# A Fourier mixing and feed-forward kernel: half-row products moved ahead of the slot's feed-forward product, one block scaled by a matmul, moved slots, and another setup

## The chip, the cores and the metric

The kernel runs on one core of one Trainium2 chip. The metric is the device time of one execution in microseconds (us), the median of several runs. Lower is better. A core has five engines that matter here: TensorE (PE in the profile; its weight loads are PEld), VectorE (DVE), ScalarE (ACT), GpSimd (POOL) and SyncE (SP), which issues DMA transfers. GpSimd issues DMA transfers too. Each engine works through its own list of instructions, and waits on semaphores where an operand comes from another engine.

## The reference, cut to what matters

Each of 8 sequences of 3008 rows and 256 features is filtered in the frequency domain. The result goes row by row through a normalization and a gated feed-forward layer of width 1536.

```python
def _attn_ref(x, filt_r, filt_i):            # x: 8 x 3008 x 256
    X = np.fft.rfft(x, axis=1)
    F = (filt_r + 1j * filt_i)[None, :, :]   # 1505 x 256
    Y = X * F
    return np.fft.irfft(Y, n=x.shape[1], axis=1)

def _moe_ref(x, w_gate, w_val, w_out, rms_g):  # x: 24064 x 256
    rms = np.sqrt(np.mean(x * x, axis=-1, keepdims=True) + 1e-06)
    xn = x / rms * rms_g
    g = xn @ w_gate                            # 256 -> 1536
    silu = g * (1.0 / (1.0 + np.exp(-g)))
    val = xn @ w_val
    return silu * val @ w_out                  # 1536 -> 256
```

## The kernel before

A transform of length 3008 = 47 x 64 is done as matmuls with constant tables: a_unit (length 64), b_unit (length 47, followed by the products with the filter), bi_unit (inverse of b) and n_unit (inverse of a, whose result is normalized). Data goes through DRAM between the units to be reordered (z_tmp between a and b, g_tmp between bi and n). Matmuls write to banks of PSUM, each a pool of one or two buffers; bank 3 and bank 0 have one buffer each.

For sequences 2 to 7 the filter products are made from half the rows at a time: s1 is one full product on VectorE (L248), then swap_unit makes two half-row products (L274 and L272) from the same PSUM bank, after which GpSimd adds the two (L278).

The units and the normalization:

```python
# the mixing of one sequence: a (first transform), b (second, with the filter), bi and n (inverse)
        pool, tag = ((psM, "mx"), (psG, "pg"), (psV, "pv"), (psB, "mb"), (psO, "po1"), (psO, "po0"))[i]
# ... cut ...
    def b_mm(b, i):
        ps = bank(3 if b else (0, 3, 4, 5)[i % 4], "psb").rearrange("p (a d) -> p a d", a=2)
# ... cut ...
    def b_unit(b, i, ps=None):
        if ps is None:
            ps = b_mm(b, i)
        f1, f2 = filt(2 * i, 2)
        if b:
            s1 = late_p["sp"].tile([P, 2, D], FP16, tag="s1", name="s1")
            s2 = late_p["sp"].tile([P, 2, D], FP16, tag="s2", name="s2")
            if b > 1:
                nc.vector.tensor_tensor(out=s1, in0=ps, in1=f1, op=ALU.mult)
                st[b]["s"][i] = (s1, s2, ps, f2)
                return
# ... cut ...
        eng = nc.vector
        if (i in (5, 8, 11, 14)) if b else (i in (3, 7, 10, 13)):
            eng = nc.gpsimd
# ... cut ...
            nc.scalar.activation(out=v, in_=ps, func=AXT.Copy)
            ps = v
        eng.tensor_tensor(out=s1, in0=ps, in1=f1, op=ALU.mult)
        eng.tensor_tensor(out=s2, in0=ps, in1=f2, op=ALU.mult)
        st[b]["s"][i] = (s1, s2)

    def swap_unit(b, i, h):
        s1, s2, ps, f2 = st[b]["s"][i]
        a, e = slice(HALF * h, HALF * h + HALF), slice(HALF - HALF * h, P - HALF * h)
        if h:
            nc.vector.tensor_tensor(out=s2[a], in0=ps[e], in1=f2[e], op=ALU.mult)
        else:
            nc.vector.scalar_tensor_tensor(out=s2[a], in0=ps[e], scalar=-1.0, in1=f2[e],
                                           op0=ALU.mult, op1=ALU.mult)
        if h:
            s = late_p["ssp"].tile([P, 2, D], FP16, tag="s", name="s")
            nc.gpsimd.tensor_tensor(out=s, in0=s1, in1=s2, op=ALU.add)
            st[b]["s"][i] = (s,)

    def bi_unit(b, i):
# ... cut ...
                nc.tensor.matmul(ps[:, u, :], wi_at(q, 2 * i + u), ss[q][:, u, :],
                                 start=(q == 0), stop=(q == n - 1))
# ... cut ...
# normalization: squares, their sum over the 256 features, 1/sqrt, broadcast over partitions
    def q_unit(b, m):
# ... cut ...
                nc.tensor.matmul(ps[:, q:q + 1], sq[:, dh, ts(q, P)], ones,
                                 start=(dh == 0), stop=(dh == 1))
# ... cut ...
        rho = up.tile([P, 4], FP32, tag="rho", name="rho")
        nc.vector.tensor_scalar(out=u[:, 0:n], in0=ps[:, 0:n], scalar1=1.0 / D, scalar2=1e-6 * Y_SCALE * Y_SCALE,
                                op0=ALU.mult, op1=ALU.add)
        nc.gpsimd.tensor_tensor(out=rho[:, 0:n], in0=u[:, 0:n], in1=mhalf[:, 0:n], op=ALU.pow)
        if b or m > 1:
            nc.gpsimd.dma_start(r_d[b, m, 0:n * P].rearrange("(p q) -> p q", q=n), rho[:, 0:n])
# ... cut ...
    def rho_load(b, m):
        rb = late_p["rp"].tile([P, 4 * P], FP32, tag="rb", name="rb")
        w = nq(b, m) * P
        nc.sync.dma_start(rb[:, 0:w], r_d[b, m, 0:w].partition_broadcast(P))
        st[b]["u"][m] = rb

    def scale_apply(m, bk):
        hl = st[0]["u"].pop(m)
        y = st[0]["y"].pop(m)
        ps = bank(bk, "psr")
        for q in range(4):
            for e in range(2):
                nc.tensor.matmul(ps[:, ts(q, P)], hl[:, e, q:q + 1].to_broadcast([P, P]), ident,
                                 start=(e == 0), stop=(e == 1))
        xn = xnp.tile([P, 2, 512], FP16, tag="xn", name="xn")
        for dh in range(2):
            nc.vector.tensor_tensor(out=xn[:, dh, :], in0=ps, in1=y[:, dh, :], op=ALU.mult)
        st[0]["xn"][m] = xn

    def xn_unit(b, m):
# ... cut ...
        nc.gpsimd.tensor_tensor(out=xv, in0=yv, in1=rv.unsqueeze(1).to_broadcast([P, 2, n, P]),
                                op=ALU.mult)
        st[b]["xn"][m] = xn
```

The feed-forward layer is a list of 576 items, 12 for each of 6 blocks of 512 rows in each of 8 sequences. gv makes the two products of an item (pg and pv), ScalarE the sigmoid-weighted sg, VectorE the product hh; down adds hh times w_out into po, two slots later:

```python
    def gv(b, m, jt):
# ... cut ...
        for ps, wt in ((pg, wg), (pv, wv)):
            for dt_ in range(2):
                nc.tensor.matmul(ps[:, 0:w], wt[:, dt_, ts(jt, P)], xn[:, dt_, 0:w],
                                 start=(dt_ == 0), stop=(dt_ == 1))
# ... cut ...
        nc.scalar.activation(out=sg[:, 0:w], in_=pg[:, 0:w], func=AXT.Silu)
        nc.vector.tensor_tensor(out=hh[:, 0:w], in0=pv[:, 0:w], in1=sg[:, 0:w], op=ALU.mult)
# ... cut ...
    def down(b, m, jt):
# ... cut ...
        for s4 in range(n):
            nc.tensor.matmul(po[s4 // 2][:, s4 % 2, :], hh[:, ts(s4, P)], wo[:, jt, :],
                             start=(jt == 0 and s4 % 2 == 0),
                             stop=(jt == JT - 1 and (s4 % 2 == 1 or s4 == n - 1)))
# ... cut ...
        if jt == JT - 1:
# ... cut ...
            nc.scalar.activation(out=o3[:, 0:2, :], in_=po[0], func=AXT.Copy)
            nc.vector.tensor_copy(out=o3[:, 2:n, :], in_=po[1][:, 0:n - 2, :])
```

Everything else is laid into the slots of these items by a plan: at slot i comes gv, then the slot's planned units, then the down product of item i - 2, then the q_units.

```python
        def at(slot, fn, *a):
            todo = (late if fn == q_unit else plan).setdefault(slot, [])
            if fn in (sq_unit, swap_unit):
                todo.insert(0, (fn, a))
            else:
                todo.append((fn, a))

        def norm_plan(b, m, s0, s1, r):
            for dh in range(2):
                at((s0, s1)[dh], n_unit, b, m, dh)
                at((s0, s1)[dh] + 1, sq_unit, b, m, dh)
            for d, fn in zip(r, (q_unit, rho_load, xn_unit)):
                at(s1 + d, fn, b, m)
# ... cut ...
            b_at = [t - 26 + 4 * i for i in range(16)]
# ... cut ...
            elif b == 2:
# ... cut ...
                b_at = [72] + [71 + 3 * i for i in range(1, 16)]
                lag, t4_at = 5, 123
                n_at = [127 + 8 * m for m in range(6)]
            elif b == 3:
# ... cut ...
            for i in range(16):
                s0 = b_at[i]
                at(s0, b_unit, b, i)
                if b > 1:
                    at(s0 + 1, swap_unit, b, i, 0)
                    at(s0 + 2, swap_unit, b, i, 1)
                at(s0 + lag - (b == 2 and i == 0), bi_unit, b, i)
                if i % 2 == 1:
                    at(s0 + lag + 1, g_store, b, i // 2)
            if b + 1 < B:
                for c in range(NXC):
                    at((24, 73)[b - 1] + 2 * c if b < 3 else a_at[3 * c + 2] + 2, x_load, b + 1, c)
# ... cut ...
        for i in range(len(items) + 4):
            if i < len(items):
                gv(*items[i])
            for fn, a in plan.get(i, ()):
                fn(*a)
            if 2 <= i < len(items) + 2:
                down(*items[i - 2])
                if items[i - 2][2] == JT - 1:
                    stores[i + 1] = items[i - 2][:2]
            for fn, a in late.get(i, ()):
                fn(*a)
            if i in stores:
                o_store(*stores[i])
```

Ahead of the slots stands a setup: tables and filters are loaded, and sequence 0 is mixed without DRAM between its units. The filter parts fr and fi (4 tiles each, c = 0 to 3) are loaded into half of the partitions and copied to the other half by f_dup. t1_unit makes transposes (pt), t2_unit too (of gT); bit_unit is the inverse of b for sequence 0 (pgt, copied to gT); n_first and y_first make the first block's normalization input.

```python
    def f_dup(c, which=(0, 1)):
        for e in which:
            t = (fr, fi)[e][c]
            a, o = (0, HALF) if e else (HALF, 0)
            if c == 3:
                nc.sync.dma_start(t[a:a + HALF], t[o:o + HALF])
            elif e:
                nc.gpsimd.tensor_copy(out=t[a:a + HALF], in_=t[o:o + HALF])
            else:
                nc.scalar.activation(out=t[a:a + HALF], in_=t[o:o + HALF], func=AXT.Copy)
# ... cut ...
        for m in range(6):
            if m == 4:
                warm_up(6, 0)
            for dh in range(2):
                at_unit(m, dh)
# ... cut ...
        ps0 = {}
        for g in range(8):
            t1_unit(g)
            if g == 1:
                ps0.update((i, b_mm(0, i)) for i in range(2))
        ps0.update((i, b_mm(0, i)) for i in range(2, 4))
        f_dup(0)
        f_dup(1, (1,))
        f_dup(3)
        for i in range(16):
            if i == 6:
                f_dup(2)
            b_unit(0, i, ps0.get(i))
            if i == 3:
                f_dup(1, (0,))
            if i % 2 and i >= 5:
                bit_unit(i - 5)
                bit_unit(i - 4)
            if i == 13:
                w_load(0)
                w_load(1)
        for i in range(12, 16):
            bit_unit(i)
        t2_unit(0, 1)
        t2_unit(1, 0)
        warm_up(2, 0)
        first = n_first()
        y_first(*first, 1)
        q_unit(0, 0)
        y_first(*first, 0)
        scale_split(0)
        t2_unit(2, 0)
        t2_unit(3, 0)
        scale_apply(0, 3)
        t2_unit(4, 0)
```

Of the kernel before, what the change touches and what calls it, by code (L numbers as in the profile page):

```python
# [12 lines left out]
AXT = mybir.ActivationFunctionType  # L13
# [109 lines left out]
def kernel(  # L123
# [105 lines left out]
    def b_mm(b, i):  # L229
        ps = bank(3 if b else (0, 3, 4, 5)[i % 4], "psb").rearrange("p (a d) -> p a d", a=2)  # L230
# [7 lines left out]
        return ps  # L238

    def b_unit(b, i, ps=None):  # L240
        if ps is None:
            ps = b_mm(b, i)
# [15 lines left out]
        if (i in (5, 8, 11, 14)) if b else (i in (3, 7, 10, 13)):  # L258
# [75 lines left out]
    def q_unit(b, m):  # L334
# [12 lines left out]
        if b or m > 1:  # L347
            nc.gpsimd.dma_start(r_d[b, m, 0:n * P].rearrange("(p q) -> p q", q=n), rho[:, 0:n])
        else:
            st[b]["u"][m] = rho  # L350
# [21 lines left out]
    def y_first(y, pss, dh):  # L372
        if dh:
            nc.scalar.activation(out=y[:, dh, :], in_=pss[dh], func=AXT.Identity, scale=gsb[:, dh:dh + 1])
            return
# [3 lines left out]
    def scale_split(m):  # L379
        rho = st[0]["u"].pop(m)  # L380
# [3 lines left out]
        st[0]["u"][m] = hl  # L384

    def scale_apply(m, bk):
        hl = st[0]["u"].pop(m)
        y = st[0]["y"].pop(m)
# [8 lines left out]
        st[0]["xn"][m] = xn  # L397
# [13 lines left out]

    hh_of = {}
# [65 lines left out]
    def f_dup(c, which=(0, 1)):  # L478
        for e in which:
            t = (fr, fi)[e][c]  # L480
            a, o = (0, HALF) if e else (HALF, 0)
            if c == 3:
                nc.sync.dma_start(t[a:a + HALF], t[o:o + HALF])
            elif e:
                nc.gpsimd.tensor_copy(out=t[a:a + HALF], in_=t[o:o + HALF])
            else:
                nc.scalar.activation(out=t[a:a + HALF], in_=t[o:o + HALF], func=AXT.Copy)
# [13 lines left out]
    def t1_unit(g):  # L501
# [7 lines left out]
        pool, tag = ((psG, "pg"), (psV, "pv"))[g % 2]  # L509
# [7 lines left out]
        if g != 1:  # L517
# [75 lines left out]
    with tc.manual_schedule():  # L593
# [26 lines left out]
        for c in range(1, 4):  # L620
            nc.vector.memset(fr[c][0:HALF], 0.0)
            zero(fi[c][HALF:P])
        with nc.allow_non_contiguous_dma(reason="one gain a partition"):
            nc.sync.dma_start(gsb, moe_rms_g.rearrange("(a p) -> p a", p=P))
        for c in range(4):
            f_load(c, filt_r, fr[c], 0, nc.sync)
            f_load(c, filt_i, fi[c], HALF, nc.gpsimd if c < 3 else nc.sync)
# [4 lines left out]
        for m in range(6):  # L632
            if m == 4:
                warm_up(6, 0)
# [4 lines left out]
        ps0 = {}  # L639
        for g in range(8):  # L640
            t1_unit(g)
            if g == 1:
                ps0.update((i, b_mm(0, i)) for i in range(2))
# [169 lines left out]
```

## Time and profile before

| | |
|---|---|
| time, median of 3 | 919.47 us (918.31 to 919.63) |
| span of the profiled run | 917.9 us |
| TensorE busy | 884.3 us, 96% |
| VectorE busy | 673.8 us, 73% |
| ScalarE busy | 618.8 us, 67% |
| GpSimd busy | 391.6 us, 43% |
| DMA | 102.22 MB, mean 111 GB/s |
| granted TensorE clock, mean | 0.991 of full |
| first pg matmul of slot 0 | 48.31 us after the span's start |

The profile counts a matmul as busy from its start to a modelled end, so that matmuls overlap one another. What a stretch must take at least is better read from the number of columns that its matmuls move, and from the start-to-start time of matmuls that wait for nothing. The start of slot n is the start of the first pg matmul of item n: slot 0 at 48.31 us, slot 71 at 168.50, slot 72 at 171.64, slot 119 at 255.41, slot 120 at 256.71.

In a line of the profile, L428 is line 428 of the kernel before, an arrow as in hh<-pv,sg has the written tile at its left, and "idle before" names what ended the engine's idle time.

### The profile page before, as it was taken

The page shows a single profiled execution, that of the slowest core. Times are in us where ns is not written, and L with a number is a line of the kernel's source. Part 1 is how long each engine was busy: PE and PEld are TensorE (multiplying, and loading weights), DVE is VectorE, ACT ScalarE, POOL GpSimd, SP SyncE. Part 2 cuts the span into 40 slices and gives each one's busy share as a digit, 9 for nine tenths or more (in the row PEclk, how much of TensorE's full clock was granted, in tenths as well). Part 3 has the DMA queues.
Part 4 walks back from the last instruction along what each step waited for, and adds up shares of the span by engine and source line. Part 5 has one row for each costly group of instructions (what it writes and reads, how often), then busy time and mean ns, then how long its engine had stood idle before and what let it go on. Part 6 is the DMA issues. An engine that isn't in the chain of part 4 may idle for free.

```text
span 917.9 us, 17521 instructions
## 1 busy us (share of the span) xinstructions
PE 884.3 (96%) x6327; PEld 560.6 (61%) x6327; DVE 673.8 (73%) x1069; ACT 618.8 (67%) x1048; POOL 391.6 (43%) x352
## 2 busy tenths in 40 slices
PE   8799999799999999999999999999999999999997
PEld 5566566455556666666666666666666666666554
DVE  7766667578888876887877886888878887555554
ACT  7667566567667776787667776687657775676543
POOL 6842730654535552366515552265514553034200
PEclk9899999999999999999999999999999999999999
DMA  9696715682663347443463455343362222331201
GB/s 194 131 189 158 154 50 181 142 176 69 144 173 80 102 99 201 101 107 91 113 183 78 98 122 137 115 117 81 81 172 70 64 64 73 94 69 53 59 24 46
DMA packets 80191, 102.22 MB, mean 111 GB/s; under 512 B 8141, under 2 KB 56653, under 8 KB 79593
## 3 DMA queue, kind: packets, MB, share of 16 engines
q1 hardware_dynamic: 69832, 85.15, 34.5%
q0 software_dynamic: 10272, 15.96, 11.2%
q8 instruction: 49, 0.80, 0.4%
q14 instruction: 38, 0.30, 0.1%
HBM read 67.93 MB, written 46.79 MB: 125 GB/s over the span
## 4 chain that ended last, share of the span: by engine, by line
PE 79%; DMA 6%; DVE 6%; issue 5%; POOL 2%; ACT 1%; SPq 0%; POOLq 0%; ACTq 0%; DVEq 0%
PE po L440 23%; PE pg L423 23%; PE pv L423 22%; DVE hh L428 3%; PE psb L237 2%; PE psi L287 2%; PE psn L319 2%; PE psa L204 2%; DVE o L446 1%; DMA fr<-in_filt_r_dram 1%; DMA r_tmp<-rho 1%; DVE s L272 1%; DMA rb<-r_tmp 1%; ACT sg L427 1%; PE psq L340 1%
## 5 line engine op out<-in xcount | busy, mean ns | idle before, releaser
L428 DVE TENSOR_TENSOR hh<-pv,sg 128x512 f16<-128x512 f32 (+1 forms) x576 | 391.7, 680 | 219.2 <-ACT sg L427 104.3
L427 ACT ACTIVATE sg<-pg 128x512 f16<-128x512 f32 (+1 forms) x576 | 338.8, 588 | 242.1 <-PE pg L423 231.8
L440 PE MATMUL po<-wo,hh 128*128 128x256 f16 x2256 | 344.4, 273 | 2.4 <-DVE o L446 0.3
L423 PE MATMUL pg<-xn,wg 128*128 128x512 f16 (+1 forms) x1152 | 338.4, 375 | 2.4 <-POOL xn L407 2.4
L423 PE MATMUL pv<-xn,wv 128*128 128x512 f16 (+1 forms) x1152 | 338.3, 375 | 0.0
L440 PEld LDWEIGHTS <-hh 128*128 128x128 f16 x2256 | 216.7, 98 | 101.0 <-issue 5.1
L278 POOL TENSOR_TENSOR s<-s,s 128x512 f16<-128x512 f16 x96 | 110.6, 1152 | 299.6 <-DVE s L272 232.8
L423 PEld LDWEIGHTS <-wv 128*128 128x128 f16 x1152 | 112.7, 98 | 131.8 <-issue 1.3
L407 POOL TENSOR_TENSOR xn<-y,rb 128x1024 f16<-128x1024 f32 (+1 forms) x46 | 128.8, 2801 | 50.5 <-DMA rb<-r_tmp 26.8
L423 PEld LDWEIGHTS <-wg 128*128 128x128 f16 x1152 | 109.1, 98 | 15.7 <-issue 3.5
L346 POOL TENSOR_TENSOR rho<-u,mhalf 128x4 f32<-128x4 f32 (+1 forms) x48 | 48.9, 1019 | 74.5 <-DVE u L344 74.3
L292 ACT ACTIVATE t<-psi 96x512 f16<-96x512 f32 x112 | 66.3, 592 | 14.5 <-PE psi L287 6.4
L325 ACT ACTIVATE y<-psn,gsb 128x512 f32<-128x512 f32 (+1 forms) x94 | 63.8, 678 | 10.1 <-PE psn L319 3.0
L274 DVE SCALAR_TENSOR_TENSOR s<-psb,fi 64x512 f16<-64x512 f32 x96 | 66.6, 693 | 3.0
L272 DVE TENSOR_TENSOR s<-psb,fi 64x512 f16<-64x512 f32 x96 | 65.7, 684 | 3.0
L248 DVE TENSOR_TENSOR s<-psb,fr 128x512 f16<-128x512 f32 x96 | 65.4, 681 | 1.0 <-PE psb L237 1.0
L331 ACT ACTIVATE sq<-psn 128x512 f16<-128x512 f32 (+1 forms) x94 | 54.8, 583 | 0.0
L237 PE MATMUL psb<-t,wb 96*128 96x256 f16 x224 | 43.2, 273 | 8.7 <-DVE s L272 4.7
L209 ACT ACTIVATE t<-psa 128x512 f16<-128x512 f32 x70 | 41.8, 597 | 8.4 <-PE psa L204 5.2
L287 PE MATMUL psi<-s,wi 128*128 128x256 f16 x248 | 45.5, 273 | 0.0
L287 PEld LDWEIGHTS <-wi 128*128 128x128 f16 x248 | 24.4, 98 | 27.0 <-issue 2.1
L319 PEld LDWEIGHTS <-t 128*128 128x128 f16 x368 | 28.5, 98 | 20.0
(96 smaller groups left out, 507.7 us busy)
## 6 DMA issues: line engine op xcount, KB each, us to landing
out_dram<-o SPq DMA_DIRECT2D x84, 256.0 KB
xc<-in_x_dram POOLq DMA_DIRECT2D x56, 192.0 KB, 5.9
z_tmp<-t SPq DMA_DIRECT2D x28, 384.0 KB
rb<-r_tmp SPq DMA_DIRECT2D x42, 256.0 KB
t<-z_tmp SPq DMA_DIRECT2D x28, 384.0 KB
g_tmp<-t SPq DMA_DIRECT2D x56, 192.0 KB
t<-g_tmp SPq DMA_DIRECT2D x21, 384.0 KB
out_dram<-o SPq DMA_DIRECT2D x12, 192.0 KB
```

The lines of the kernel that those rows point to most:

```text
L248: nc.vector.tensor_tensor(out=s1, in0=ps, in1=f1, op=ALU.mult)
L272: nc.vector.tensor_tensor(out=s2[a], in0=ps[e], in1=f2[e], op=ALU.mult)
L274: nc.vector.scalar_tensor_tensor(out=s2[a], in0=ps[e], scalar=-1.0, in1=f2[e], op0=ALU.mult, op1=ALU.mult)
L278: nc.gpsimd.tensor_tensor(out=s, in0=s1, in1=s2, op=ALU.add)
L287: nc.tensor.matmul(ps[:, u, :], wi_at(q, 2 * i + u), ss[q][:, u, :], start=(q == 0), stop=(q == n - 1))
L292: nc.scalar.activation(out=st[b]["t3"][c][:, 2 * r:2 * r + 2, :], in_=ps[0:KR], func=AXT.Copy)
L325: nc.scalar.activation(out=y[:, dh, 0:w], in_=ps[:, 0:w], func=AXT.Identity, scale=gsb[:, dh:dh + 1])
L407: nc.gpsimd.tensor_tensor(out=xv, in0=yv, in1=rv.unsqueeze(1).to_broadcast([P, 2, n, P]), op=ALU.mult)
L423: nc.tensor.matmul(ps[:, 0:w], wt[:, dt_, ts(jt, P)], xn[:, dt_, 0:w], start=(dt_ == 0), stop=(dt_ == 1))
L427: nc.scalar.activation(out=sg[:, 0:w], in_=pg[:, 0:w], func=AXT.Silu)
L428: nc.vector.tensor_tensor(out=hh[:, 0:w], in0=pv[:, 0:w], in1=sg[:, 0:w], op=ALU.mult)
L440: nc.tensor.matmul(po[s4 // 2][:, s4 % 2, :], hh[:, ts(s4, P)], wo[:, jt, :], start=(jt == 0 and s4 % 2 == 0), stop=(jt == JT - 1 and (s4 ...
```

## The change

It has four parts.

- In the slots' plan, swap_unit gets a list of its own, which is worked ahead of gv. The two half-row products of a unit then stand ahead of the slot's hh product in VectorE's list, not behind it.
- Sequence 1's block 0 is scaled as blocks 0 and 1 of sequence 0 are: 1/rms is split into two fp16 parts and broadcast over the partitions by matmuls with the identity, and VectorE multiplies. Before, it went to DRAM, came back broadcast by DMA, and GpSimd multiplied.
- Units are moved: the first b_unit of sequence 2 from slot 72 to 71, that of sequence 3 from 118 to 119, the loads of x for sequence 3 from slots 73, 75, 77, 79 to 68, 75, 82, 89.
- The setup is another: the b products of sequence 0 aren't begun during the t1 transposes, which now use the same four banks as the b products; t1's copies go to VectorE for 5 of 8 units and to ScalarE for 3; six warm-up matmuls are gone; the copies of filter halves are all made by GpSimd (tiles 0 and 1, and fi of tile 3) and ScalarE (tile 2, and fr of tile 3), none by DMA; GpSimd takes three b_units (4, 8, 11) and not four (3, 7, 10, 13); both halves of the first block's y are made on VectorE, and one more t2 copy.

```diff
--- before.py
+++ after.py
@@ -255,7 +254,7 @@
         eng = nc.vector
-        if (i in (5, 8, 11, 14)) if b else (i in (3, 7, 10, 13)):
+        if (i in (5, 8, 11, 14)) if b else (i in (4, 8, 11)):
             eng = nc.gpsimd
@@ -344,7 +343,7 @@
         nc.gpsimd.tensor_tensor(out=rho[:, 0:n], in0=u[:, 0:n], in1=mhalf[:, 0:n], op=ALU.pow)
-        if b or m > 1:
+        if (b, m) not in by_matmul:
             nc.gpsimd.dma_start(r_d[b, m, 0:n * P].rearrange("(p q) -> p q", q=n), rho[:, 0:n])
@@ -370,22 +369,19 @@
     def y_first(y, pss, dh):
-        if dh:
-            nc.scalar.activation(out=y[:, dh, :], in_=pss[dh], func=AXT.Identity, scale=gsb[:, dh:dh + 1])
-            return
         nc.vector.tensor_scalar(out=y[:, dh, :], in0=pss[dh], scalar1=gsb[:, dh:dh + 1],
... (scale_split and scale_apply take the sequence b as an argument)
@@
+    by_matmul = ((0, 0), (0, 1), (1, 0))
@@ -475,16 +472,12 @@
 
-    def f_dup(c, which=(0, 1)):
-        for e in which:
-            t = (fr, fi)[e][c]
-            a, o = (0, HALF) if e else (HALF, 0)
-            if c == 3:
-                nc.sync.dma_start(t[a:a + HALF], t[o:o + HALF])
-            elif e:
-                nc.gpsimd.tensor_copy(out=t[a:a + HALF], in_=t[o:o + HALF])
+    def f_dup(c):
+        for t, a, e in ((fr[c], HALF, 0), (fi[c], 0, HALF)):
+            if c == 2 or (c == 3 and a):
+                nc.scalar.activation(out=t[a:a + HALF], in_=t[e:e + HALF], func=AXT.Copy)
             else:
-                nc.scalar.activation(out=t[a:a + HALF], in_=t[o:o + HALF], func=AXT.Copy)
+                nc.gpsimd.tensor_copy(out=t[a:a + HALF], in_=t[e:e + HALF])
@@ -506,7 +499,7 @@
         st[0]["t2"][g] = dst
-        pool, tag = ((psG, "pg"), (psV, "pv"))[g % 2]
+        pool, tag = ((psO, "po0"), (psO, "po1"), (psM, "mx"), (psB, "mb"))[g % 4]
         ps = pool.tile([P, 4, D], FP16, tag=tag, name="pt1")
@@ -514,7 +507,7 @@
                 nc.tensor.transpose(ps[:, a, ts(dh, P)], src, ident)
-        if g != 1:
+        if g % 2 == 0 or g == 7:
             nc.vector.tensor_copy(out=dst, in_=ps[0:KR])
@@ -620,41 +613,36 @@
             zero(fi[c][HALF:P])
+        for c in range(4):
+            f_load(c, filt_r, fr[c], 0, nc.sync)
+            if c < 3:
+                f_load(c, filt_i, fi[c], HALF, nc.gpsimd)
         with nc.allow_non_contiguous_dma(reason="one gain a partition"):
             nc.sync.dma_start(gsb, moe_rms_g.rearrange("(a p) -> p a", p=P))
-        for c in range(4):
-            f_load(c, filt_r, fr[c], 0, nc.sync)
-            f_load(c, filt_i, fi[c], HALF, nc.gpsimd if c < 3 else nc.sync)
 
         for m in range(6):
-            if m == 4:
-                warm_up(6, 0)
             for dh in range(2):
                 wi_group(g)
-        ps0 = {}
-        for g in range(8):
-            t1_unit(g)
-            if g == 1:
-                ps0.update((i, b_mm(0, i)) for i in range(2))
-        ps0.update((i, b_mm(0, i)) for i in range(2, 4))
+        for i in range(8):
+            t1_unit(i)
         f_dup(0)
-        f_dup(1, (1,))
-        f_dup(3)
+        f_load(3, filt_i, fi[3], HALF, nc.gpsimd)
+        f_dup(1)
         for i in range(16):
-            if i == 6:
-                f_dup(2)
-            b_unit(0, i, ps0.get(i))
-            if i == 3:
-                f_dup(1, (0,))
+            if i == 7:
+                f_dup(3)
+            b_unit(0, i)
             if i % 2 and i >= 5:
                 bit_unit(i - 4)
-            if i == 13:
+            if i == 4:
+                f_dup(2)
+            if i == 11:
                 w_load(0)
@@ -663,13 +651,13 @@
         first = n_first()
-        y_first(*first, 1)
         q_unit(0, 0)
         y_first(*first, 0)
-        scale_split(0)
-        t2_unit(2, 0)
+        scale_split(0, 0)
+        y_first(*first, 1)
+        t2_unit(2, 1)
         t2_unit(3, 0)
-        scale_apply(0, 3)
+        scale_apply(0, 0, 3)
         t2_unit(4, 0)
@@ -694,11 +682,11 @@
         items = [(b, m, jt) for b in range(B) for m in range(6) for jt in range(JT)]
-        plan, late = {}, {}
+        pre, plan, late = {}, {}, {}
 
         def at(slot, fn, *a):
-            todo = (late if fn == q_unit else plan).setdefault(slot, [])
-            if fn in (sq_unit, swap_unit):
+            todo = {q_unit: late, swap_unit: pre}.get(fn, plan).setdefault(slot, [])
+            if fn == sq_unit:
                 todo.insert(0, (fn, a))
@@ -707,14 +695,15 @@
                 at((s0, s1)[dh] + 1, sq_unit, b, m, dh)
-            for d, fn in zip(r, (q_unit, rho_load, xn_unit)):
-                at(s1 + d, fn, b, m)
+            steps = (q_unit, rho_load, xn_unit)
+            if (b, m) in by_matmul:
+                steps = (q_unit, scale_split, scale_apply)
+            for d, fn in zip(r, steps):
+                at(s1 + d, fn, b, m, *((3,) if fn == scale_apply else ()))
 
             at(j - 6, t2_unit, j, 1, 1)
-        norm_plan(0, 1, 0, 2, (2,))
-        at(6, scale_split, 1)
-        at(8, scale_apply, 1, 3)
+        norm_plan(0, 1, 0, 2, (2, 4, 6))
         at(6, open_late)
@@ -735,10 +724,11 @@
                 on_dve = (0, 1, 3, 5, 7, 8, 9, 10, 11)
-                b_at = [72] + [71 + 3 * i for i in range(1, 16)]
+                b_at = [71 + 3 * i for i in range(16)]
                 lag, t4_at = 5, 123
             elif b == 3:
+                b_at[0] += 1
                 a_at = [77, 78, 80, 81, 83, 84, 92, 93, 101, 102, 104, 105]
@@ -753,12 +743,12 @@
                     at(s0 + 2, swap_unit, b, i, 1)
-                at(s0 + lag - (b == 2 and i == 0), bi_unit, b, i)
+                at(s0 + lag - (b == 3 and i == 0), bi_unit, b, i)
                 if i % 2 == 1:
                 for c in range(NXC):
-                    at((24, 73)[b - 1] + 2 * c if b < 3 else a_at[3 * c + 2] + 2, x_load, b + 1, c)
+                    at((24 + 2 * c, 68 + 7 * c)[b - 1] if b < 3 else a_at[3 * c + 2] + 2, x_load, b + 1, c)
             for c in range(4):
@@ -768,6 +758,8 @@
         for i in range(len(items) + 4):
+            for fn, a in pre.get(i, ()):
+                fn(*a)
             if i < len(items):
... (cuts: renamings, and lines of context)
```

## The prediction

> **What bounds the kernel now.** I read the page's shares first (TensorE 96% busy), then a table of four stretches, then who TensorE waited for in each, and last single instructions. The table of stretches gives per engine the busy time and number of instructions, then the granted TensorE clock:
>
> ```profile
> core 0: us, PE busy (x) PEld busy (x) DVE busy (x) ACT busy (x) POOL busy (x), PEclk, DMA share, GB/s
> 0.00:48.31 48.31, 37.35 (x436) 27.54 (x436) 36.46 (x62) 34.11 (x49) 37.07 (x46) 0.92 0.81 163
> 48.31:168.50 120.19, 115.16 (x828) 73.69 (x827) 76.87 (x132) 80.12 (x140) 40.74 (x44) 0.98 0.62 145
> 168.50:256.71 88.21, 78.41 (x521) 47.33 (x518) 68.60 (x107) 55.03 (x94) 48.61 (x48) 1.00 0.61 135
> 256.71:917.90 661.19, 653.35 (x4552) 412.06 (x4549) 491.83 (x771) 449.53 (x766) 265.21 (x216) 1.00 0.39 98
> ```
>
> The reader sees a setup of 48.3 us, and a last stretch of 661 us in which TensorE is busy 99%. There two 512-column matmuls start 0.434 us apart (2.36 columns per ns), and 12 slots without extra work take 15.82 us, the 12 x 1.30 of their own matmuls and 0.2 more. From slot 120 on nothing but fewer matmuls could save more than some 5 us. The third stretch, slots 71 to 118, is the loose one. Its matmuls are 193 of 256 columns, 192 of 512 and 4 of 384 for the feed-forward; 64 of 256, 14 of 512 and 24 of 128 for the mixing; 30 of one column at 25 ns. That is 176,000 columns / 2.36 per ns + 0.75 us = 75.3 us of work in 88.2 us: 12.9 us lost. The same sum gives 9.6 us lost in slots 0 to 70.
>
> TensorE's waits in that third stretch, with total, times and longest:
>
> ```profile
> PE psb L237 <- DVE s L272: 4.7, 6, 2.4
> PE pg L423 <- POOL xn L407: 2.0, 1, 2.0
> PE psi L287 <- POOL s L278: 1.2, 1, 1.2
> PE psa L204 <- DMA xc<-in_x_dram: 0.8, 1, 0.8
> ```
>
> and the instructions on TensorE at which they fall (start, duration, idle before in brackets):
>
> ```profile
> 171.64 0.59 PE L423 MATMUL pg<-xn,wg 128*128 128x512 f16 x2 [2.00 <-POOL xn L407]
> ...
> 177.68 0.39 PE L237 MATMUL psb<-t,wb 96*128 96x256 f16 x2 [2.41 <-DVE s L272]
> ...
> 181.90 0.27 PE L287 MATMUL psi<-s,tb 128*128 128x256 f16 x1 [1.23 <-POOL s L278]
> ...
> 184.57 0.38 PE L204 MATMUL psa<-xc,tb 128*128 128x512 f16 x1 [0.78 <-DMA xc<-in_x_dram]
> ```
>
> After that every third slot (each b_unit of sequence 2) is 0.3 to 0.55 us long over its work. VectorE's order shows why:
>
> ```profile
> 190.12 0.68 DVE L248 TENSOR_TENSOR s<-psb,fr 128x512 f16<-128x512 f32 x1
> 191.59 0.69 DVE L428 TENSOR_TENSOR hh<-pv,sg 128x512 f16<-128x512 f32 x1 [0.79 <-PE psa L204]
> 192.31 0.69 DVE L274 SCALAR_TENSOR_TENSOR s<-psb,fi 64x512 f16<-64x512 f32 x1
> 193.11 0.69 DVE L428 TENSOR_TENSOR hh<-pv,sg 128x512 f16<-128x512 f32 x1
> 193.83 0.68 DVE L272 TENSOR_TENSOR s<-psb,fi 64x512 f16<-64x512 f32 x1
> ```
>
> VectorE idles 0.79 us for the hh product while both half-row products, whose input has long been there, stand behind hh. The second ends at 194.5 and only then may psb's single bank be written again.
>
> The setup's chain (start, duration) runs through the filters:
>
> ```profile
> 26.17 5.97 DMA fi<-in_filt_i_dram
> 32.28 5.26 DMA fi<-fi
> 37.64 1.28 POOL sg L264
> 38.91 1.23 POOL hh L265
> 40.61 1.26 ACT gT L539 x3
> ```
>
> [...] Here the half clock was granted for 6.8 us in setup and twice for 3.4 us, at 47.4 and at 115.7, after stretches with TensorE working a third of the time or less. [...] all sixteen of L272 in this stretch took 683 to 685 ns, with GpSimd busy or not.
>
> **Part 1, half-row products first.** swap_unit moves ahead of gv in its slot. No instruction is added. In the lines above the first product would fill the idle time before hh and the second follow that hh, from 192.3 to 193.0 in place of 193.8 to 194.5; TensorE asks for the bank 0.3 us before the end it now has, so it would not wait. VectorE's load per three slots is 3 x 0.69 + 0.68 + 2 x 0.69 = 4.2 us against at least 4.35 us of TensorE, so it keeps up; the hh behind a product comes up to 0.5 us later, and its reader stands two slots on. Excess in slots 80 to 116 now: .34 .34 .41 .27 .30 .55 .30 .34 .56 .30 .48 = 4.2 us. I leave 0.4 near the output copies: -3.8. From sequence 3 on units are four slots apart and the excess is zero already. The slot after an output copy is 0.29 us long there, eleven times with swaps near it; VectorE's backlog ahead of that copy is some 0.15 us shorter: 11 x 0.15 = 1.6, of which I count -1.0.
>
> **Part 2, sequence 1 block 0 by matmul broadcast.** Out go one store of 2 KB, its broadcast load, and 2.85 us of GpSimd. In come 8 matmuls of 128 columns (0.43 us on TensorE), two splits of 0.16 us and two products of 0.65 us on VectorE (1.29 for two in setup). xn is then ready some 1.5 us into slot 68 and slot 72 does not wait: slot 71's 2.16 us go, 0.43 come: -1.7.
>
> **Part 3, moved slots.** b_unit 0 of sequence 2 at 71 instead of 72: now its second product and the next unit's psb share slot 74, which costs the 2.41 us wait (2.59 with the slot's rest): -2.6. b_unit 0 of sequence 3 goes from 118, the slot of sequence 2's last half-row product, to 119: 1.64 us go. x(3) is asked for from slot 68 on instead of 73: the 0.78 us wait and the 0.16 beside it go: -0.9. The psi wait at slot 76 (1.38 us over) hangs on GpSimd, which did xn of block 1 (176.76 to 179.6), x(3) and then s. With one xn, one load and x(3) gone from in front, rho of block 1 still starts at 164.67, but its store no longer shares the queues with the t2 loads, as these go out a slot or two earlier; I put its round trip at 6 us in place of 10.8, s near 176.3, and psi just met: -0.8, the most doubtful term here.
>
> Sum of the loop: -3.8 - 1.0 - 1.7 - 2.6 - 1.6 - 0.9 - 0.8 = -12.4 us.
>
> **Part 4, setup.** Removed: the early b products, 6 warm-up matmuls, two copies of 512 KB by DMA, one GpSimd unit. GpSimd now: copies of fr0 and fi0 (1.9 each) till 23.0, the load of fi3 issued by 24.8, copies of fr1 and fi1 to 28.6, unit 4 (2.5) to 31.1, copy of fi3 to 33.0, units 8 and 11. ScalarE: three t1 copies (1.0 each) to 23.0, fr2 and fi2 copies (1.95 each, fr2 landing near 26.2) to 30.1, two gT (0.9), fr3 to 32.9, two gT, then unit 8's copy near 34.4; GpSimd's unit 8 therefore ends at 36.9 and unit 11 at 39.4. VectorE starts units at 23.8 instead of 24.9, though it has 13 in place of 12: 13 x 1.2 us and a wait of some 0.3 end near 39.8. Before, the last unit ended at 40.1. But then bits 11 to 15 are left instead of 13 to 15: last gT near 42.2 instead of 41.9 (+0.3). Then y's second half and one t2 copy (0.68 and 0.42 us) move from ScalarE to VectorE, between the split and the xn products; the products can start 0.5 us later: +0.5. Setup: +0.8 us.
>
> Sum: 919.5 - 12.4 + 0.8 = 907.9. Terms of this kind come in rather short than over, so I say 909.
>
> **Rivals.** (a) VectorE becomes the bound: products ahead of hh delay hh, and the down product waits. For it: VectorE is at 68.6 of 88.2 us and rises to some 69.9 of 77. Against it: two slots of slack. It would leave 3 to 4 us of the gain unmade: 912. (b) GpSimd's chain of rho, store, load and xn of block 1 is as late as before, and psi at 76 or the first block still waits: 2 to 3 us less gain, 911. (c) Setup is really worse: the t1 copies now share four single banks with the b products, and without the warm-up the clock may halve during the 64 transposes (4.2 us at full clock). That costs up to 4 us more: 912 to 913. (d) Setup gains, as the DMA copies' 5.26 us leave its chain: up to 3 us better, 905.
>
> **Range and chances.** (a) to (c) together would make about 915, (d) with all terms 904: range 904 to 915. For over 2% faster, under 901.1, the loop would have to lose almost nothing; 0.04. Over 2% slower needs a new stall of 20 us: 0.02.
>
> **What would show it.** Part 1: waits of psb on L272 at zero, sum of TensorE's waits in slots 71 to 118 at 1 us or less. Part 2: no pg wait on xn at slot 72. Part 3: psb at slot 74, psa at 77 and psb of sequence 3 without wait; psi at 76 under 0.6 us. Part 4: the first pg near 49.1 in place of 48.3, and GpSimd's last setup unit near 39.4. I am wrong if slot 120 starts less than 8 us earlier, or if setup moves by over 2 us either way.

## The result and the profile after

The changed kernel takes 904.94 us (median of 4 runs, 904.51 to 907.15), beside 918.89 us for the kernel before (918.26 to 919.63). The ratio is 0.985, with a 95% interval of 0.983 to 0.987: 12 to 15 us were saved, where the prediction had 10.5.

The first view is again the table of four stretches, now of the changed kernel. The stretches begin at the first pg matmul of slots 0, 71 and 120, so that they hold the same slots as in the table of the kernel before.

```profile
core 0: us, PE busy (x) PEld busy (x) DVE busy (x) ACT busy (x) POOL busy (x), PEclk, DMA share, GB/s
0.00:50.59 50.59, 37.50 (x429) 27.62 (x430) 37.73 (x64) 34.29 (x48) 40.46 (x50) 0.89 0.74 146
50.59:167.80 117.21, 114.08 (x837) 73.81 (x836) 77.99 (x136) 80.34 (x140) 40.79 (x44) 0.99 0.61 146
167.80:245.28 77.48, 75.49 (x521) 47.48 (x518) 67.47 (x106) 55.00 (x94) 44.16 (x45) 1.00 0.65 146
245.28:903.30 658.02, 651.67 (x4552) 412.10 (x4549) 493.71 (x772) 449.69 (x766) 265.95 (x216) 1.00 0.39 99
```

Against the table before: setup +2.3 us, slots 0 to 70 -3.0, slots 71 to 119 -10.7, the rest -3.2. Three of these four are not what the prediction had: setup was to cost 0.8, slots 0 to 70 were to stay as they were, and the rest was to give 1.0.

TensorE's waits in the third stretch (total, times, longest) are down to two lines:

```profile
PE psi L286 <- POOL s L277: 1.6, 1, 1.6
PE po L437 <- DVE o L443: 0.4, 1, 0.4
```

They fall at slots 74 and 76, as TensorE's timeline shows (start, duration, idle before):

```profile
173.26 0.38 PE L437 MATMUL po<-wo,hh 128*128 128x256 f16 x2 [0.41 <-DVE o L443]
177.38 0.27 PE L286 MATMUL psi<-s,tb 128*128 128x256 f16 x1 [1.58 <-POOL s L277]
```

The waits of psb on the half-row product, of pg on xn and of psa on x are gone; that of psi on GpSimd is still there, 1.58 us beside 1.23. VectorE's timeline in the same place of the plan as in the prediction:

```profile
189.44 0.68 DVE L247 TENSOR_TENSOR s<-psb,fr 128x512 f16<-128x512 f32 x1
190.14 0.69 DVE L273 SCALAR_TENSOR_TENSOR s<-psb,fi 64x512 f16<-64x512 f32 x1
190.86 0.69 DVE L425 TENSOR_TENSOR hh<-pv,sg 128x512 f16<-128x512 f32 x1
191.59 0.68 DVE L271 TENSOR_TENSOR s<-psb,fi 64x512 f16<-64x512 f32 x1
192.30 0.69 DVE L425 TENSOR_TENSOR hh<-pv,sg 128x512 f16<-128x512 f32 x1
```

No line has idle time in it. The second half-row product ends 2.83 us after the full product began; before, it was 4.39 us (190.12 to 194.51).

To compare kernels of which some start slot 0 later than others I use one measure throughout: **the lost time** of a stretch, its span less the columns of its matmuls at 2.36 per ns (the prediction's rate, with its 25 ns for a matmul of one column). "From 120" is counted up to the start of the last slot. Here it is in us for the kernel before, the changed one and the experiments on the four parts. "Alone" means one part put into the kernel before.

| kernel | slot 0 starts | lost in 0-70 | of it slots 37, 38 | lost in 71-79 | lost in 80-119 | lost from 120 |
|---|---|---|---|---|---|---|
| before | 48.3 | 9.6 | 4.1 | 7.1 | 6.0 | 5.0 |
| changed | 50.6 | 6.2 | 0.9 | 2.3 | 0.0 | 2.0 |
| changed, a second trace | 50.8 | 6.9 | 1.1 | 2.3 | 0.0 | 2.0 |
| half rows first, alone | 47.9 | 8.8 | 3.1 | 7.3 | 0.6 | 1.4 |
| changed, half rows behind | 50.0 | 6.9 | 2.2 | 2.7 | 4.7 | 5.9 |
| block 0 by matmul, alone | 48.3 | 7.7 | 2.1 | 4.6 | 6.0 | 5.0 |
| b_units moved, alone | 48.0 | 9.1 | 3.4 | 9.9 | 4.7 | 5.7 |
| b_units and x loads moved, alone | 49.4 | 6.5 | 1.7 | 7.3 | 4.7 | 5.7 |
| new setup, alone | 49.9 | 9.2 | 4.1 | 7.8 | 6.0 | 4.9 |
| changed, old setup | 50.1 | 7.4 | 2.8 | 4.8 | 0.0 | 1.8 |

Some of this lost time is not waiting but half clock. In these traces the granted TensorE clock falls to half for pieces of 3.41 us (in the setup also two or three of them on end: 6.8 us in the kernel before, 10.2 in the changed one), and matmuls that fill such a piece lose 1.7 us: in the kernel before two matmuls of 512 columns took 0.86 us inside the piece at 115.7 (from 117.08 to 117.94) and 0.43 us behind it (from 119.81 to 120.24). Here is one in the kernel with only block 0 by matmul (columns as in the table of stretches):

```profile
170.51:173.92 3.41, 1.10 (x7) 0.36 (x4) 3.16 (x6) 1.25 (x3) 3.41 (x3) 1.00 0.17 59
173.92:177.34 3.42, 3.32 (x12) 1.80 (x13) 0.78 (x3) 0.60 (x1) 2.56 (x4) 0.50 0.82 187
```

In each trace these pieces lie on one grid of 3.41 us (in the kernel before they begin at 26.96, 47.44 and 115.7 us, 6 and 20 times 3.41 apart). Of the grid's stretches that begin after slot 0, end before the last matmuls and run at full clock, in all fourteen traces, seven were followed by half clock; their matmul columns filled 0.19 to 0.29 of them at the full rate. All others were filled to 0.41 or more. (The prediction's "a third of the time or less" is 0.21, 0.33 and 0.29 by this measure; by the profile's busy time, with its modelled ends, it is 0.30, 0.52 and 0.34.) In the setup, stretches of up to 0.41 were followed by half clock too, so no threshold comes out of this. The same wait of 2.41 us at slot 74 was followed by half clock here and not in the kernel before, where the stretch that held it was filled to 0.41. So a trace can lose 1.7 us more or less with the same waits. In the column for slots 71 to 79, 1.7 us are half clock with the order alone (slots 72 and 73), block 0 alone (74 and 75), both rows of moved b_units (77 and 78) and the old setup (77 and 78), and nothing in the others; in slots 37 and 38, 1.7 us are half clock before and with the new setup alone.

### The profile page after: what moved, and what is told of

It is laid out like the page before. It is cut to its first block, busy times and chain, and to the rows that moved or that the text cites. A ratio compares the mean times of both kernels' runs of the same rounds, so it can differ in the third digit from the quotient of the medians.

```text
span 903.3 us, 17520 instructions
## 1 busy us (share of the span) xinstructions
PE 878.7 (97%) x6329; PEld 561.0 (62%) x6329; DVE 676.9 (75%) x1075; ACT 619.3 (69%) x1047; POOL 391.4 (43%) x353
## 3 DMA queue, kind: packets, MB, share of 16 engines
q0 software_dynamic: 10384, 16.35, 11.4%
## 4 chain that ended last, share of the span: by engine, by line
PE 86%; issue 5%; DMA 3%; DVE 2%; POOL 2%; ACT 2%; SPq 0%; POOLq 0%; ACTq 0%
PE po L437 25%; PE pg L420 25%; PE pv L420 25%; PE psi L286 3%; PE psb L241 3%; PE psn L318 2%; DMA fr<-in_filt_r_dram 2%; PE psa L204 2%; PE psq L339 1%; DVE o L443 1%; DMA rb<-r_tmp 1%; POOL xc L189 0%; DVE hh L425 0%; ACT fr L478 0%; ACT sg L424 0%
## 5 line engine op out<-in xcount | busy, mean ns | idle before, releaser
L403 POOL TENSOR_TENSOR xn<-y,rb 128x1024 f16<-128x1024 f32 (+1 forms) x45 | 126.1, 2802 | 46.7 <-DMA rb<-r_tmp 32.8
```

## The experiments

Theory: the four parts act nearly by themselves, the order on VectorE is the largest of them, and setup costs what the others partly hide. Rivals: the moved slots carry much of the gain, as the prediction had it; or the parts are needed together; or the unpredicted gain in slots 0 to 70 belongs to the new setup. Every ratio below is against the kernel before, run beside it on the same chip, with its 95% interval.

### The order on VectorE

Alone, on the kernel before:

```diff
-            todo = (late if fn == q_unit else plan).setdefault(slot, [])
-            if fn in (sq_unit, swap_unit):
+            todo = {q_unit: late, swap_unit: pre}.get(fn, plan).setdefault(slot, [])
+            if fn == sq_unit:
...
+            for fn, a in pre.get(i, ()):
+                fn(*a)
             if i < len(items):
                 gv(*items[i])
```

> The kernel before with only the half-row products ahead of the slot's hh product. From the two traces: the excess of 4.2 us in slots 80 to 116 and the eleven excesses of 0.29 us after output copies go, some of the 2.4 us wait at slot 74 and the 1.6 us at slot 118 go too, as the product ahead of hh frees the bank sooner: -8 to -10 us, near 910. Rival, that VectorE's order matters only together with the moved slots: under 5 us.

Measured: 910.28 us, ratio 0.990 (0.988 to 0.992), so -8.9 us. And the opposite, the same lines taken back in the changed kernel:

```diff
-            todo = {q_unit: late, swap_unit: pre}.get(fn, plan).setdefault(slot, [])
-            if fn == sq_unit:
+            todo = (late if fn == q_unit else plan).setdefault(slot, [])
+            if fn in (sq_unit, swap_unit):
```

> The changed kernel with the half-row products behind the slot's hh product again. If the order is worth what the two traces show (4.2 us in slots 80 to 116, 3.1 us after output copies), the time is 904.9 + 7.3 = 912. If the moved slots alone had removed the waits, 905 to 907.

Measured: 915.65 us, ratio 0.996 (0.995 to 0.998); 10.7 us more than the changed kernel's 904.94, which was measured on another chip, and some 10 by the two ratios. In the traces the lost time differs from the changed kernel's by 0.4 us in slots 71 to 79, 4.7 in 80 to 119 and 3.9 from 120 on.

The waits of TensorE from 167 to 250 us, slots 71 to 119, with the order alone (same columns as above) show what it takes and what it leaves:

```profile
PE pg L423 <- POOL xn L407: 2.4, 1, 2.4
PE psi L287 <- POOL s L278: 1.6, 1, 1.6
PE psb L237 <- DVE s L272: 0.8, 2, 0.5
PE psa L204 <- DMA xc<-in_x_dram: 0.6, 1, 0.6
```

psb's wait on the half-row product falls from 4.7 us in six times to 0.8 in two, with the b_units where they were. Slot 74 goes from 2.6 us lost to 0.6, slot 118 from 1.6 to 0.6. Both had been given to the moved b_units in the prediction. Two units' psb do meet in slot 74, as it says, but with the products ahead of hh the meeting costs little.

### Block 0 of sequence 1 scaled by matmul

Alone, on the kernel before:

```diff
-        if b or m > 1:
+        if (b, m) not in by_matmul:
...
+    by_matmul = ((0, 0), (0, 1), (1, 0))
...
+            steps = (q_unit, rho_load, xn_unit)
+            if (b, m) in by_matmul:
+                steps = (q_unit, scale_split, scale_apply)
```

> The kernel before with only sequence 1 block 0 scaled by matmul. Prediction's part 2 by itself: slot 71 (2.2 us over) is met, 0.43 us of matmuls come, so -1.7, near 917.4. Rival: the stall at slots 74 to 77 stands behind the same transfers and only grows by what slot 71 gives up, so the time is within 0.5 us of before.

Measured: 915.79 us, ratio 0.996 (0.995 to 0.997), -3.5 us. Slot 71 loses nothing (2.2 before) and slot 76 nothing (1.4 before); slots 74 and 75 lose 1.6 more, all of it half clock. So part of its gain is where the prediction didn't look: GpSimd, spared one xn, is in time for the psi of slot 76. That didn't hold in the whole change, where this wait stayed. GpSimd's timeline in the changed kernel says what it waited for:

```profile
173.35 2.87 POOL L403 TENSOR_TENSOR xn<-y,rb 128x1024 f16<-128x1024 f32 x1 [3.03 <-DMA rb<-r_tmp]
176.18 1.15 POOL L277 TENSOR_TENSOR s<-s,s 128x512 f16<-128x512 f16 x1
```

The xn of block 1 waits 3.03 us for its broadcast load, issued at 166.81 and landed just ahead of 173.35; s stands behind it, and psi behind s. With block 0 by matmul alone, block 1's load took only 4.1 us (issued at 166.34, xn at 170.42). A difference between the two is the change's own part 3: GpSimd now issues the first two loads of x for sequence 3 at 165.38, between block 1's store (164.74) and its load; with block 0 alone they came at 173.22, after xn. From the store's issue to xn it took 6.5 us with block 0 alone, and 8.2 to 9.4 in the five traces in which the x loads stand between. That these loads hold it up fits, and wasn't tried by itself. If the wait for block 1's load is the cause, block 1 by matmul as well must remove the wait:

```diff
-    by_matmul = ((0, 0), (0, 1), (1, 0))
+    by_matmul = ((0, 0), (0, 1), (1, 0), (1, 1))
...
-                          (2, 6, 10) if b > 1 else (2, 5, 8))
+                          (2, 6, 10) if b > 1 else (2, 4, 6) if m == 1 else (2, 5, 8))
```

> The changed kernel with sequence 1 block 1 scaled by matmul too (split at slot 68, applied at slot 70). If slot 76 waits (1.7 us over in the changed kernel, up to 2.5 in others) because GpSimd stands in the product of block 1, whose broadcast load is late, then that wait goes and 0.43 us come: -1.2 to -1.6 us, near 903.5. Rival, that GpSimd's sum is late for another reason: slot 76 stays over 1 us and the time is 905 or more.

Measured: 904.85 us, ratio 0.984 (0.982 to 0.986). In the trace slot 76 loses nothing and slots 71 to 79 lose 0.7 us in place of 2.3; 0.4 us of matmuls come in. The cause holds. The time, against 904.94 for the changed kernel on another chip, doesn't show the gain: 903.5 was expected.

### The moved slots

The two b_units moved, alone, on the kernel before:

```diff
-                b_at = [72] + [71 + 3 * i for i in range(1, 16)]
+                b_at = [71 + 3 * i for i in range(16)]
...
             elif b == 3:
+                b_at[0] += 1
...
-                at(s0 + lag - (b == 2 and i == 0), bi_unit, b, i)
+                at(s0 + lag - (b == 3 and i == 0), bi_unit, b, i)
```

> The kernel before with only the two moved b_units (sequence 2's first from slot 72 to 71, sequence 3's first from 118 to 119). Part 3 by itself, with the order of the products as before: the 2.6 us at slot 74 shrink to under 1 and the 1.6 us at 118 go: -3, near 916. Rival, that swap-first does the same work alone (it took slot 74 to 0.6 and slot 118 to 0.6 us over): the same -3 here, but then the two parts overlap and their gains don't add in the changed kernel.

Measured: 920.02 us, ratio 1.001 (0.999 to 1.003): no difference that can be told. TensorE's waits from 167 to 250 us in this kernel:

```profile
PE psa L204 <- DMA xc<-in_x_dram: 2.5, 1, 2.5
PE psi L287 <- POOL s L278: 2.5, 1, 2.5
PE psb L237 <- DMA t<-z_tmp: 1.5, 1, 1.5
PE psb L237 <- DVE s L272: 1.3, 4, 0.8
```

The 2.4 us wait at slot 74 has shrunk to 0.8, and TensorE waits for the next things instead: for x (2.5, before 0.8), for GpSimd (2.5, before 1.2) and for the z_tmp load (1.5, before none). Slots 71 to 79 lose 9.9 us in place of 7.1, of which 1.7 are half clock. So the x loads were moved as well, which is the whole of the prediction's part 3:

```diff
-                    at((24, 73)[b - 1] + 2 * c if b < 3 else a_at[3 * c + 2] + 2, x_load, b + 1, c)
+                    at((24 + 2 * c, 68 + 7 * c)[b - 1] if b < 3 else a_at[3 * c + 2] + 2, x_load, b + 1, c)
```

> The kernel before with the whole of part 3: both b_units moved and the loads of x for sequence 3. Moved b_units alone gave nothing: what they saved at slots 74 and 118 came back at slots 76 to 78, with 2.5 us waiting for x(3) and 2.5 us for GpSimd's sum. If the load at slot 68 takes the first of these away, -2 to -3, near 916.5. If the x load merely trades places with the broadcast load of block 1 in the queues, within 1 us of before.

Measured: 917.72 us, ratio 0.999 (0.998 to 1.000), -0.8 us and not told from nothing. The wait for x is gone; slots 71 to 79 lose 7.3 us, 1.7 of them at half clock, beside 7.1 before, so that 1.5 us of waits did go in this trace. Slot 118 loses nothing (1.6 before), and 0.7 us come at slot 122. The x loads moved without the b_units weren't tried, nor either move taken back in the changed kernel.

### The setup

The setup of the kernel before put into the changed one, in its main lines:

```diff
-        for i in range(8):
-            t1_unit(i)
+        ps0 = {}
+        for g in range(8):
+            t1_unit(g)
+            if g == 1:
+                ps0.update((i, b_mm(0, i)) for i in range(2))
+        ps0.update((i, b_mm(0, i)) for i in range(2, 4))
... (and f_dup, the GpSimd units, warm_up, y_first of before)
```

> The changed kernel with the setup of before. Theory A, setup time adds to the end: slot 0 starts near 48.3 us instead of 50.6, and the time is 904.9 - 2.3 = 902.6. Theory B, the later start was hidden by transfers that got a head start on the slots: slot 0 starts near 48.3, but the 3 us stall of slot 37 (b_unit waiting for ScalarE, which waits for a g_tmp store) is back, and the time is 905 to 906. Rival to both, the stall of slot 37 is chance: it comes or stays away whatever the setup.

Measured: 907.17 us (904.88 to 908.22), ratio 0.986 (0.984 to 0.989): not told from the changed kernel. Its trace isn't that of a shorter setup either: slot 0 starts at 50.1, psi at slot 76 waits longer (2.5 us lost there), and half clock follows. The reverse, the new setup put into the kernel before (the same edit the other way):

> The kernel before with the setup of after, nothing else of the change. Theory A: slot 0 near 50.6, time 919 + 2.3 = 921. Theory B: slot 0 near 50.6, the stall of slot 37 under 0.5 us, and the time 918 to 919, no worse than before.

Measured: 920.70 us, ratio 1.002 (1.0005 to 1.003): the new setup costs 1.6 us (0.5 to 2.8). Over the traces of the study slot 0 starts at a median of 48.3 us with the old setup (47.9 to 50.1, seven kernels) and 50.1 with the new one (49.6 to 50.8, seven kernels). The loss in slots 37 and 38 is 4.1 us with the new setup alone, as before: the gain there isn't the setup's. Where the time in setup goes, VectorE's timeline of the changed kernel shows:

```profile
35.93 0.69 DVE L263 TENSOR_TENSOR ss<-psb,fr 128x512 f16<-128x512 f32 x1 [2.32 <-POOL ss L263]
```

VectorE idles 2.32 us ahead of b_unit 12. The psb that it reads was begun on TensorE at 35.11, behind the inverse products (pgt) of units 6 and 7, and these wait for ScalarE, as TensorE's waits in the setup say:

```profile
PE pgt L523 <- ACT gT L532: 2.8, 2, 1.6
```

ScalarE has the gT copies behind its copies of filter halves (at 26.57, 28.50 and 31.18, 1.9 us each). The line names a GpSimd product as the releaser, as it ended at nearly the same time; that unit 12 waits for its psb is read from the order of TensorE's instructions and wasn't tried by itself.

The clock has a share in it. In this trace it is half from 32.8 to 43.0 us. In the trace of the new setup alone it is full from 21.4 to 38.5: the gT copy at 33.1 comes at the same time, but psb of unit 12 begins at 34.66 and VectorE's last product ends at 40.7, not 41.5. Ahead of slot 0 half clock was granted for 8.0 to 15.7 us in the seven traces with the new setup and for 4.0 to 10.2 in the seven with the old one; the 22 runs of the new setup alone had a mean granted clock of 0.988, beside 0.992 for the kernel before. Whether the six warm-up matmuls that are gone bring this wasn't tried, so how much of the 1.6 us is the clock's stays open.

### Slot 37

Before, TensorE lost 3.1 us at slot 37 and 1.0 at slot 38, of which 1.7 are half clock after a wait of 2.39 us; in the changed kernel 0.0 and 0.8. No part of the change touches these slots. ScalarE's timeline of the kernel before, where the time was lost:

```profile
114.72 0.59 ACT L292 ACTIVATE t<-psi 96x512 f16<-96x512 f32 x1 [3.01 <-DMA g_tmp<-t]
115.21 0.58 ACT L262 ACTIVATE v<-psb 128x512 f32<-128x512 f32 x1
```

The first copy needs a buffer that the g_tmp store is still reading; v, for which TensorE's psb waits, stands behind. That store was late because of SyncE's order (SPq is its queue of transfers):

```profile
105.82 0.33 SPq L355 DMA_DIRECT2D rb<-r_tmp  x1
...
107.82 0.48 SPq L295 DMA_DIRECT2D g_tmp<-t  x1
```

and SyncE's waits from 96 to 112 us in the same kernel:

```profile
SPq L355 <- DMA r_tmp<-rho: 8.3, 1, 8.3
```

SyncE stood 8.3 us at the broadcast load of block 5's 1/rms, which waited for its own store, with the g_tmp store behind it. If this is the cause, the load put four slots later must free slot 37 in every trace:

```diff
-            norm_plan(0, m, s0, s0 + 2, (2, 5, 8))
+            norm_plan(0, m, s0, s0 + 2, (2, 9, 12) if m == 5 else (2, 5, 8))
```

> The changed kernel with one broadcast load (sequence 0 block 5, not needed before slot 60) asked for at slot 34 instead of 30. If slot 37's stall, 0 to 3.1 us in the six traces so far, comes from a g_tmp store that stands behind this load in SyncE's list, slot 37 is met in the trace and the median falls by 1 to 2 us to 903 to 904, with less spread. Rival, that the store is slow by itself in the crowded queues: slot 37 goes on varying and the median stays at 905.

Measured: 905.74 us, ratio 0.986 (0.983 to 0.988). The expected 903 to 904 didn't come; the changed kernel's own traces lose at most 0.2 us at slot 37, so there was little to win. SyncE's timeline now has the store first:

```profile
105.89 0.30 SPq L294 DMA_DIRECT2D g_tmp<-t  x1
107.06 0.34 SPq L354 DMA_DIRECT2D rb<-r_tmp  x1
```

Slot 37 loses nothing in all three kernels with this edit. In the eleven traces without it the slot lost 3.1 and 3.1 us (kernel before, new setup alone), 2.5, 2.2, 1.9, 1.3, 1.3, 0.9, 0.6 (the other experiments), and 0.0 and 0.2 (the changed kernel, twice). One reason for the low end can be read from the traces: the changed kernel asks for the buffer at 113.8 us, the kernel before at 111.7, as slot 0 started 2.3 us later, while SyncE gets to the g_tmp store at 107.64 and 107.82. Between these two traces the store moved by 0.2 us while slot 0 moved by 2.3, so a late start is partly taken back here. It isn't the whole: the kernels that start late lost between 0.0 and 3.1. What sets the landing in each is left open.

### Together

The changed kernel once more, with no edit, beside the next two on one chip:

> The changed kernel once more, to stand beside the next two on the same chip: 905, between 904 and 907, slot 37 and slot 76 over by 0 to 3 us each.

Measured: 905.92 us (905.67 to 906.25), ratio 0.985 (0.984 to 0.987). Block 1 by matmul and the later load together (both diffs above):

> The changed kernel with sequence 1 block 1 scaled by matmul and the broadcast load of sequence 0 block 5 asked for at slot 34. Slots 37, 74 and 76 are met in the trace; loss in slots 0 to 143 near 6 us. If the waits of the transfer chains are what is left, 902 to 903, 2 us under the changed kernel beside it. If the waits only move elsewhere, 904 to 905.

Measured: 902.67 us (902.11 to 903.87), ratio 0.982 (0.981 to 0.983), 3.2 us under the changed kernel on the same chip. And the same with the setup of before:

> As the last one, with the setup of before. In the traces so far slot 0 starts at 48.25 in the middle with the old setup (5 traces) and at 50.02 with the new one (5). With slot 37 met whatever the setup, nothing is left to hide that: 1.8 us less than the last one, near 900.5 to 901.5. If the later start is hidden in slots 0 to 36 too (transfers with a head start), no difference.

Measured: 901.85 us (901.33 to 902.19), ratio 0.981 (0.980 to 0.982), the shortest of the study. Against the kernel with the new setup the intervals overlap: the setups aren't told apart here. The third stretch of this last kernel, from its table of stretches:

```profile
core 0: us, PE busy (x) PEld busy (x) DVE busy (x) ACT busy (x) POOL busy (x), PEclk, DMA share, GB/s
...
166.28:242.17 75.89, 75.47 (x522) 47.45 (x519) 68.25 (x107) 55.02 (x94) 41.34 (x44) 1.00 0.58 135
...
```

TensorE is busy 75.5 of 75.9 us. Most of what is left to win stands in the setup and in the 5.9 us lost in slots 0 to 70.

## Why the prediction was right, and where its terms were not

The range of 904 to 915 around 909 holds 904.94 near its low end. What bounds the kernel was read rightly: the loose stretch was slots 71 to 118, of the 14.6 us between the two profiled spans 11.4 are made by the start of slot 120, and TensorE's own columns are the floor from slot 0 on. By steps:

- **Part 1, the order: mechanism right, size wrong.** Predicted -4.8; alone -8.9 (-10.8 to -7.1), and taken back 10 to 11. The term for slots 80 to 116 was right (4.3 us lost in slots 80 to 117 before, none after). "Of which I count -1.0", for the slots after output copies, was mis-sized: all eleven excesses (0.22 to 0.29 us each) went, about -3.1, and the lost time from slot 120 on fell from 5.0 to 1.4 with the order alone. And the order also takes 2.0 us at slot 74 and 1.0 at slot 118, which the prediction had put down to the moved slots. Its sum for VectorE's load, 4.2 us in three slots, is 4.13; nothing hangs on that.
- **Part 2, block 0 by matmul: right, too small.** Predicted -1.7, alone -3.5 (-4.7 to -2.5). Slot 71's 2.16 us went as said. In that experiment GpSimd's relief freed slot 76 too; 2.0 us less at slots 37 and 38 and 1.7 more of half clock at slots 74 and 75 are of the kind that varies from trace to trace.
- **Part 3, moved slots: wrong.** Predicted -5.9; alone -0.8, with an interval that holds zero. The term -2.6 took slot 74's wait for lost time that would not come back; moved alone, the b_units turned it into waits for x, GpSimd and z_tmp at slots 76 and 77, and half clock behind them. -2.6 and -1.6 had been counted as if the order weren't there, though part 1 shortens the same wait. In the whole change the moves do take the rest: slot 118 loses 0.6 us with the order alone and nothing in the changed kernel, slot 77 0.8 and nothing. How much of the total that is wasn't tried in that setting.
- **psi at slot 76, -0.8: failed.** "I put its round trip at 6 us" gave the store and load of block 1 too little: from the store's issue at 164.74 to xn at 173.35 it took 8.6 us, of which the load alone took 6.5. s ended at 177.33, psi could have begun at 175.80, and it waited 1.58 us. Rival (b) was true; block 1 by matmul showed it. With block 0 alone the round trip did take 6.5 us and psi didn't wait, so the term may have missed what its own x loads at slot 68 cost.
- **Part 4, the setup: +0.8 predicted, +1.6 (0.5 to 2.8) alone.** GpSimd's terms held (unit 11 ended at 39.5; 39.4 said). The failed term is VectorE's "a wait of some 0.3": unit 12 waited 2.32, VectorE's last unit ended at 41.5 in place of 39.8, and the first pg came at 50.59 in place of 49.1. (Its "Before, the last unit ended at 40.1" is GpSimd's end; VectorE's last product ended at 40.7.) By the prediction's own test, setup moving by over 2 us, it was wrong here in the profiled run. Rival (c) named the clock, and half clock is longer with the new setup; but in the changed kernel it came after the transposes, which ran at full clock (4.4 us). In two traces, the new setup alone and the changed kernel's second, it fell on the transposes, which then took 5.8 and 6.3 us. Rival (d), a shorter setup, didn't come.
- **Rival (a)** showed as small as it can: one po matmul in slot 74 waits 0.41 us for an output copy behind VectorE's products, and another in slot 122 0.26.
- **Not in the prediction:** 3.3 us less lost at slots 37 and 38 between the two profiled runs, 1.7 of them half clock. It offset the setup there.

So the total was met because errors cancelled: the order and the matmul were worth more than said (-12.4 alone, against -6.5), the moved slots less (-0.8 against -5.9). The four parts alone sum to -8.9 - 3.5 - 0.8 + 1.6 = -11.6 us, against -12.6 to -14.0 for the whole in two comparisons: nearly additive. The 1 to 2.4 us between are no more than the intervals of the four allow, so that anything is made only together isn't shown.

## What to carry to other kernels

When one wait is cured in a plan of slots, the next wait in the same slots decides what is gained: give each slot's excess to one part only, and ask of every part what the other parts leave of it. An instruction whose input is long there, standing behind one whose input is not, cost far from where it stands here, 0.22 to 0.29 us at each of eleven output copies later in the run; look for idle time on an engine with ready work behind it in its list, as VectorE's 0.79 us in the prediction. The same showed on SyncE, which stood 8.3 us at one load: a load that waits for its own store belongs behind stores that others wait for. And compare single traces only after taking out what the clock took: here one stall in one trace, and not in the next, brought 3.4 us of half clock.

## What the runs showed of the hardware

- A store of at most 2 KB and a broadcast load of at most 256 KB took over 6 us each. The store of block 5's 1/rms was issued at 99.41 in the kernel before and landed 6.4 us later, when its load went at 105.82; the core's DMA moved 228 GB/s in between. Block 1's load was issued at 166.81 in the changed kernel, and the xn that waited for it began 6.5 us later, at 155 GB/s.
- A half-row product over 64 partitions took 0.68 to 0.69 us on VectorE, as long as the full product over 128 (0.68): the two halves together took 1.37 us.
